# Keeping a twelfth chunk of each row in SBUF between the two layers of a decode attention kernel

## The chip, the core and the metric

The kernel runs on one core of one Trainium2 chip, in one launch. The metric is the device time of that core in microseconds (us), the median of several executions. Less is better.

## What is computed

Two rounds of the same two layers, A then B, on eight rows (a batch of 8, one token each) of 448 numbers. Both rounds of A use the same weights and the same caches.

```python
def _A_ref(x, k_cache, v_cache, wq, wo):        # x 8x1x448, caches 8 x 8 x 4096 x 256
    q = (x @ wq).reshape(B, Sq, 16, 256)...      # 16 query heads, 8 cache heads
    scores = einsum("bhqd,bhkd->bhqk", q, k) * 256 ** -0.5
    p = softmax(scores)
    o = einsum("bhqk,bhkd->bhqd", p, v)
    return o... @ wo
x = x + A(layernorm(x)); x = x + B(layernorm(x))   # B: two small matmuls, gelu, an MLP
x = x + A(layernorm(x)); x = x + B(layernorm(x))
```

Everything is bf16. The caches dominate: 32 MiB for the eight heads of one row, K and V together, 256 MiB for all rows, and each of the two rounds needs all of it. The second round of a row can only begin when the first round of that row, A and B, is done; rows do not depend on each other.

## The kernel before

**Chunks.** A row's heads are taken in four pairs (`gp` 0 to 3). A pair's K is cut into four chunks of 1 MiB, and so is its V: 32 chunks to a row and pass, 512 uses of chunks in all. A chunk is [128 partitions x 4096 bf16]. The first round is pass 0 (`ps == 0`), the second pass 1.

**Places.** SBUF has `NC = 15` places of a chunk's size (one tile, `places_t`, line 76). Every chunk lies in one of them from the issue of its load to its last use.

**Kept chunks.** The list `kept` (lines 63 and 64) names the chunks of each row that stay in their place after their use in pass 0 and are used again in pass 1 without a load: all four K chunks of pairs 3 and 2, and V chunks 1, 2 and 3 of pair 3. That is eleven. Two more are kept outside the places: V chunk 1 of pair 2 (`inner`, line 65) is moved to PSUM by transposes (`away`, line 745) and brought back in pass 1 (`back`, line 752), and a quarter of V chunk 0 of pair 3 (`part`, line 66) lies in PSUM too, so that this load is 768 KB in pass 1.

**Order of the work.** `tasks` (lines 528 to 544) lists pass, row and pair by hand. Row by row it goes: the pairs 3 and 2 of pass 1, in which the kept chunks are used up; then work on other pairs mixed with pairs 2 and 3 of the next row's pass 0, whose chunks now take the places that came free; then the remaining pairs of pass 1 and pairs 0 and 1 of pass 0 of the row after that. `items` (lines 555 to 564) makes one item of each chunk's use: the K chunks of a task alternate with the V chunks of the task before it. `flushed` puts the last four V chunks together before the next row's pass 1 begins.

**Work on a chunk.** For K (lines 876 to 924): DVE transposes it in place in three instructions (`transpose_k`, line 708), and PE computes the scores (`scores`, line 715), 32 matmuls with 128 columns. If both chunks of a couple lie in places next to each other and neither has to be waited for, one set of 32 matmuls with 256 columns does both (`paired`, line 588). ACT takes the exponential (line 737). For V (lines 925 to 960): 16 matmuls into the output bank (`pv`, line 776). Between the items, `step` (line 838) does a piece of the small work of finished rows: softmax sums, output projection, MLP, the next query.

**Loads.** `loads` (line 578) holds the items that need a load, in the order of use: all but the kept and inner ones of pass 1. After each item, the place of its chunk is given back (`places.append`, line 975), unless the chunk stays, and `emit_loads` (line 660) issues as many of the next loads as there are free places, from SP's queue. `place_for` and `both_for` choose the place: for K chunks of a couple they look for two places side by side and may hold one of them back; couples that land in one are loaded by one DMA of 2 MiB (line 675), all others by one of 1 MiB (line 700). Eight semaphores serve the DMAs in turn, so at most eight are under way.

Of the kernel before, what the change touches and what calls it, by code (L numbers as in the profile page):

```python
# [17 lines left out]
def kernel(  # L18
# [37 lines left out]
    GP = G // 2  # L56
# [4 lines left out]
    NC = 15  # L61

    kept = [(gp, 0, n) for gp in (GP - 1, GP - 2) for n in range(4)]
    kept += [(GP - 1, 1, n) for n in range(1, 4)]
    inner = (GP - 2, 1, 1)
    part = (GP - 1, 1, 0)
    Q4 = 4 * Dh
# [791 lines left out]
    for idx, it in enumerate(items):  # L859
# [7 lines left out]
        n, kv, c = it  # L867
# [181 lines left out]
```

## Time and profile before

| | |
|---|---|
| runs | 1097.26, 1099.54, 1105.74 us; median 1099.54 |
| profiled execution | span 1093.6 us from the first to the last instruction; the page gives no other time for it |
| busy, share of the span | PE 62%, weight loads 41%, DVE 55%, ACT 12%, POOL 1% |
| granted TensorE clock | 0.593 of full speed on average |
| moved by DMA | 446.80 MB, 444.32 of it on SP's queue, 1.93 MB in 118 packets of instructions |
| loads of V chunks | 215 of 1024 KB, 8 of 768 KB, 2 of 512 KB |
| loads of K chunks | 146 of 1024 KB, 23 of 2048 KB |
| SP waits before V and K loads for | DVE transposes 203.7 us, PE's V matmuls 180.0 us, PE's score matmuls 102.3 us, landings of V 110.1 us and of K 87.0 us |

A profile here is one execution as the hardware's profiler recorded it. Its page gives the busy time of each engine, and, in 40 equal slices, the busy share of each engine in tenths and what the DMA engines moved. The trace behind it can be asked for any stretch of time, for each issue of a DMA and its landing, and for what ended each wait. PE is TensorE (PEld its weight loads), DVE is VectorE, ACT ScalarE, SP the engine whose queue issues the loads. A line number such as L713 is one of the kernel. When SP waits before a load, the name behind it is the work that had to end first: the last reader of the chunk that was in the place, or the landing of an earlier DMA of the same semaphore.

In the last 30 us of the span the loads have ended; the last chunk lands at 1080.7 us, and the rest is the end of the last row and the output.

### The profile page before, as it was taken

Reading aid. Unit: us, or ns where it says so; the run is one execution under the profiler, and the core shown is the slowest. Engines: PE = TensorE matmul, PEld = TensorE weight load, DVE = VectorE, ACT = ScalarE, POOL = GpSimd, SP = SyncE. Lnnn points to the kernel's source line nnn. Section 1 sums busy time; section 2 is a strip of 40 time slices with the busy share of each in tenths; the row PEclk is TensorE's granted clock in tenths of the full one; section 3 lists DMA queues with packets and bytes.
Section 4 is the critical chain, followed back from the end, with each engine's and each line's share of the span. In section 5 each row is a group of like instructions: output and inputs, shape, how many; then the busy total and the mean of one; then the engine's idle time right before and its main releaser. Section 6 shows DMA issues by size and latency. Waiting matters only on the chain. (4 is left out here: it accounts for less than half of the span.)

```text
span 1093.6 us, 32866 instructions
## 1 busy us (share of the span) xinstructions
PE 674.9 (62%) x15063; PEld 451.8 (41%) x15063; DVE 599.1 (55%) x1215; ACT 125.9 (12%) x362; POOL 16.3 (1%) x27
## 2 busy tenths in 40 slices
PE   3234568456864677446774467834776477767775
PEld 2123345334642355324552245522454244545554
DVE  4256564656366555555465564665637553585462
ACT  0001101110110111101021001201111101111110
POOL 0000000000000000000000000000000000000000
PEclk9986556655575556555566555665556555665565
DMA  9999999999999999999999999999999999999994
GB/s 356 394 427 419 416 403 420 420 416 407 418 423 419 406 417 422 423 419 402 419 422 423 420 401 418 423 421 417 411 416 421 420 398 419 421 411 409 421 417 188
DMA packets 62010, 446.80 MB, mean 409 GB/s; under 512 B 6568, under 2 KB 10544, under 8 KB 12336
## 3 DMA queue, kind: packets, MB, share of 16 engines
q1 hardware_dynamic: 61680, 444.32, 98.6%
q8 instruction: 118, 1.93, 0.7%
q10 hardware_dynamic: 192, 0.38, 0.2%
q14 instruction: 20, 0.16, 0.0%
HBM read 444.67 MB, written 0.01 MB: 407 GB/s over the span
## 5 line engine op out<-in xcount | busy, mean ns | idle before, releaser
L713 DVE STREAM_TRANSPOSE places<-places 128x512 uint32<-128x512 uint32 (+1 forms) x576 | 462.0, 858 | 263.1 <-DMA places<-in_A_k_cache_dram 262.7
L728 PE MATMUL sc<-places,qbd 128*8 128x128 bf16 (+1 forms) x6720 | 281.9, 309 | 217.8 <-DVE places L713 179.7
L783 PE MATMUL o<-places,ptw 128*8 128x256 bf16 x3968 | 241.9, 387 | 144.6 <-DMA places<-in_A_v_cache_dram 122.1
L728 PEld LDWEIGHTS <-qbd 128*8 128x8 bf16 x6720 | 161.2, 101 | 312.8 <-issue 136.8
L783 PEld LDWEIGHTS <-ptw 128*8 128x8 bf16 x3968 | 114.1, 109 | 192.2 <-issue 151.0
L737 ACT ACTIVATE p_n<-sc 128x256 bf16<-128x256 f32 x128 | 95.6, 747 | 763.1 <-PE sc L728 763.1
L309 PEld LDWEIGHTS <-wq_sb 128*128 128x128 bf16 x1152 | 36.0, 104 | 28.3 <-issue 18.4
L358 PEld LDWEIGHTS <-wo_sb 128*128 128x128 bf16 x1280 | 38.4, 102 | 19.8 <-issue 19.8
L332 DVE CAST qbd<-misc 32x64 bf16<-32x64 f32 x64 | 13.8, 216 | 55.6 <-PE misc L328 55.0
L309 PE MATMUL misc<-xb,wq_sb 128*128 128x1 bf16 x1024 | 34.5, 166 | 6.2 <-ACT ptw L771 3.2
L358 PE MATMUL misc<-OT,wo_sb 128*128 128x1 bf16 x1024 | 34.5, 165 | 1.2 <-issue 1.2
L737 ACT ACTIVATION_READ_ACCUMULATOR p_n<-sc 128x1 f32 x128 | 33.9, 265 | 0.0
L771 ACT CAST ptw<-misc 128x128 bf16<-128x128 f32 x64 | 17.4, 273 | 139.1 <-PE misc L764 79.1
L463 PEld LDWEIGHTS misc<-R,o_sb 128*128 128x128 f32 x124 | 26.1, 292 | 9.4 <-issue 8.6
L247 POOL TENSOR_TENSOR t<-t,nhalf 128x2 f32<-128x2 f32 (+2 forms) x20 | 14.0, 703 | 1064.9 <-DVE t L268 1064.9
L463 PE MATMUL misc<-R,o_sb 128*128 128x8 f32 x124 | 28.8, 342 | 0.1
L431 PE MATMUL misc<-zm,one 128*128 128x8 f32 (+1 forms) x66 | 18.5, 354 | 15.0 <-DVE zm L423 14.2
L755 DVE STREAM_TRANSPOSE places<-store 128x512 uint32<-128x512 uint32 x32 | 20.1, 684 | 10.7 <-PE sc L728 10.6
L431 PEld LDWEIGHTS misc<-zm,one 128*128 128x128 f32 x66 | 16.0, 300 | 21.5 <-issue 15.8
L376 PEld LDWEIGHTS <-w_sb 128*128 128x128 bf16 x560 | 17.2, 105 | 9.4 <-issue 9.2
L376 PE MATMUL misc<-xb,w_sb 128*128 128x1 bf16 (+1 forms) x560 | 18.5, 166 | 3.6 <-DVE xb L286 2.2
L748 DVE STREAM_TRANSPOSE store<-places 128x512 uint32<-128x512 uint32 x32 | 19.9, 690 | 0.9 <-DMA places<-in_A_v_cache_dram 0.8
(103 smaller groups left out, 241.9 us busy)
## 6 DMA issues: line engine op xcount, KB each, us to landing
places<-in_A_v_cache_dram SPq DMA_DIRECT2D x215, 1024.0 KB, 9.5
places<-in_A_k_cache_dram SPq DMA_DIRECT2D x146, 1024.0 KB, 9.9
places<-in_A_k_cache_dram SPq DMA_DIRECT2D x23, 2048.0 KB, 18.7
places<-in_A_v_cache_dram SPq DMA_DIRECT2D x8, 768.0 KB, 7.2
wo_sb<-in_A_wo_dram SPq DMA_DIRECT2D x1, 3584.0 KB, 27.5
wq_sb<-in_A_wq_dram SPq DMA_DIRECT2D x3, 1024.0 KB, 8.0
w_sb<-in_B_w_dram SPq DMA_DIRECT2D x1, 1568.0 KB
w_sb<-in_B_w_dram SPq DMA_DIRECT2D x3, 448.0 KB, 26.2
```

The source lines that it names most:

```text
L309: nc.tensor.matmul(q_ps[:, j * Hq + h, :], w, xbs(nb)[:, xi, :], start=(fc == 0), stop=(fc == 3),)
L358: nc.tensor.matmul(y_ps[:, fc, :], w[:, i, at : at + 128], rhs(i), start=start, stop=stop, skip_group_check=open is not None,)
L376: nc.tensor.matmul(h_ps[:, c * nb : c * nb + nb], w, xbs(nb)[:, xi, :], start=(fc == 0), stop=(fc == 3),)
L431: nc.tensor.matmul(z_ps, ones, zm[:], start=True, stop=True)
L463: nc.tensor.matmul(ot_ps[:, j], o_sb[:].rearrange("p (i j) -> p j i", j=2)[:, j], R[:], start=True, stop=True)
L713: nc.vector.transpose(w, w)
L728: nc.tensor.matmul(sc[32 * k : 32 * k + 8, 128 * x : 128 * (x + nx)], qbd[:, ep, gp].rearrange("p a h -> p (a h)"), v, start=(n == 0), sto ...
L737: nc.scalar.activation(p_sb[:, :, :, 2 * u : 2 * u + 2].rearrange("p t i x -> p x t i"), sc[:, 256 * u : 256 * u + 256].rearrange("p (x t ...
L748: nc.vector.transpose(store[n][:].bitcast(U32), slot[:].bitcast(U32)[:, 512 * n : 512 * n + 512])
L755: nc.vector.transpose(slot[:].bitcast(U32)[:, 512 * n : 512 * n + 512], store[n][:].bitcast(U32))
L771: nc.scalar.copy(ptw[:, :, :, 6:8], pt_ps.rearrange("p t k (a h) -> p a (t k) h", a=4),)
L783: nc.tensor.matmul(o_ps[32 * q : 32 * q + 8, :], ptz[:, at : at + 8], v[:, y * Dh : (y + 1) * Dh], start=False, stop=(y >= 12), skip_group ...
```

## The change

V chunk 2 of pair 2 joins the list of kept chunks. For each row it stays in its place from its use in pass 0 to its use in pass 1, and its load in pass 1 is left out. While a row's kept chunks are all there, three of the fifteen places are left for all other chunks instead of four. The lists of tasks and items are the same; the planner assigns places by the same rules to one load fewer for each row.

```diff
     kept = [(gp, 0, n) for gp in (GP - 1, GP - 2) for n in range(4)]
-    kept += [(GP - 1, 1, n) for n in range(1, 4)]
+    kept += [(GP - 1, 1, n) for n in range(1, 4)] + [(GP - 2, 1, 2)]
     inner = (GP - 2, 1, 1)
     part = (GP - 1, 1, 0)
```

## The prediction

> **What bounds the kernel now.** I read three views in this order: the page's slices of time, busy time by stretches, and the DMA issues with their time to landing. The slices first:
>
> ```profile
> DMA  9999999999999999999999999999999999999994
> GB/s 356 394 427 419 416 403 420 420 416 407 418 423 419 406 417 422 423 419 402 419 422 423 420 401 418 423 421 417 411 416 421 420 398 419 421 411 409 421 417 188
> DMA packets 62010, 446.80 MB, mean 409 GB/s; under 512 B 6568, under 2 KB 10544, under 8 KB 12336
> ```
>
> The DMA engines are busy from the first slice to the last but one. No engine of the core is (PE 62%, DVE 55%). So the time is bytes over rate, plus a head and a tail, and a byte not loaded is worth its full transfer. The stretches show where this holds only just:
>
> ```profile
> 300.00:368.00 68.00, 36.08 (x802) 23.25 (x790) 41.14 (x63) 8.31 (x23) 0.00 (x0) 0.63 1.01 421
> 368.00:428.00 60.00, 44.73 (x994) 30.73 (x998) 31.54 (x79) 7.36 (x22) 1.25 (x2) 0.53 1.01 412
> 428.00:500.00 72.00, 35.64 (x766) 22.00 (x755) 43.10 (x65) 8.22 (x23) 0.00 (x0) 0.57 1.01 421
> 500.00:560.00 60.00, 46.15 (x970) 30.78 (x971) 30.65 (x78) 7.65 (x23) 1.26 (x2) 0.52 1.01 411
> ```
>
> The last figure is GB/s, the one before it the DMA share. Each row of the batch has a loose stretch (421) and a tight one (411 to 412). In the tight one all eleven kept chunks are resident and the stream turns in four places. The issues of the same two kinds, from issue to landing, first 375 to 406 us (tight), then 443 to 475 us (loose):
>
> ```profile
> places<-in_A_v_cache_dram SPq DMA_DIRECT2D x7, 1024.0 KB, 8.1
> places<-in_A_k_cache_dram SPq DMA_DIRECT2D x5, 1024.0 KB, 7.3
> ...
> places<-in_A_v_cache_dram SPq DMA_DIRECT2D x5, 1024.0 KB, 23.2
> places<-in_A_k_cache_dram SPq DMA_DIRECT2D x3, 1024.0 KB, 21.2
> ```
>
> Chunks land 2.49 us apart (1 MiB at 421 GB/s), so 21 to 23 us is a queue of eight, and 7.3 is one of three: the fourth place holds the chunk being worked on. How long it is held, for a K chunk that landed at 393.13:
>
> ```profile
> 393.15 2.43 DVE L713 STREAM_TRANSPOSE places<-places 128x1024 uint32<-128x1024 uint32 x3 [1.53 <-DMA places<-in_A_k_cache_dram]
> 395.64 0.39 PE L728 MATMUL sc<-places,qbd 128*8 128x128 bf16 x8 [0.21 <-DVE places L713]
> 396.06 0.33 SPq L700 DMA_DIRECT2D places<-in_A_k_cache_dram  x1
> ```
>
> Three transposes, the last eight score matmuls, and at 396.06 SP issues the next load into the place: 2.93 us after landing. The tight stretches' K chunks give 2.93 to 3.03 nearly always; V chunks 1.1 to 2.9, mostly 2.0 to 2.4.
>
> **The change, removed work.** The chunk (pair 2, V, 2) of each row is no longer loaded in the second pass: 8 loads of 1 MiB, 8.39 MB. The fifteen stretches into which I cut 125 to 1012 us move 408 to 422 GB/s; at 416 that is 20.2 us. The eight SP issues of 0.33 us lie beside transfers and are worth nothing. The 16 matmuls that read the chunk stay. If the gain were all, the time would be 1099.5 - 20.2 = 1079.3.
>
> **The change, one place less.** From the chunk's first use to its second the stream turns in three places instead of four. With four, a load issued at release has until 9.96 us after the old chunk's landing (4 x 2.49); with three, until 7.47. For a place that held K, 7.47 - 2.94 = 4.53 us remain. How long does a 1 MiB load take with nothing ahead of it? The best row is the load issued at 150.19, late because the K chunk before it was held 4.55 us. In the trace its semaphore counts once for each of the 16 DMA engines: twelve had run dry and report 4.37 to 4.83 us after the issue, the other four, still busy, 5.33 to 6.27. A chunk is there when the last of 16 is, so I take 4.85, a little over the last dry one; the low bound is 4.45, near the first of them. Then a K place is late by 2.94 + 4.85 - 7.47 = 0.32 us. A V place held 2.3 us is not late (7.15).
>
> Being late by 0.32 shifts all that follows, and this gives the next K place its time back: with loads counted in order, the one three after a K chunk pays, the one two later just makes it, the next pays again. So I charge every second K. Going through the 16 alternating chunks of the stretch from 368 us with their own hold times, I get 0.39 + 3 x 0.31 = 1.3 us. There are eight such stretches: 10.7 us. The K chunk held 4.55 us in row 0 costs another 1.6 once. Sum 12.3. With 4.45 in place of 4.85 it is about 2 (1.5 once, and little else); if every K pays, 8 x 8 x 0.32 + 1.6 = 22.
>
> The Trainium skill ("DMA: Bandwidth & Descriptors", section "Anatomy of one DMA") puts a DMA at about 2.0 us plus bytes over 436 GB/s, fitted on another issue path; for 1 MiB I estimate 4.4 us from it. That is the first dry engine's row, not the last's: by the rule the K place would be in time and the total would be near 1081, by the row it is late.
>
> **The change, less room for uneven engines.** The page counts 118 instruction packets of 16 KB. Such a packet goes to one of the 16 DMA engines and costs it about two data packets, 2 x 0.311 = 0.62 us. Landings after one come 2.67 to 2.88 us apart instead of 2.49. With four places the engines may drift apart by 9.96 - 2.94 - 4.45 = 2.6 us before those in front run dry, so most of this is absorbed: in the tight stretches landings average 2.52. With three places they are held together within 0.1 us, and a late engine delays all. About five packets fall on the alternating part of each stretch; I take 0.35 each (the landing steps of 0.2 to 0.4), 1.75, less 0.5 paid already (16 x 0.03): 1.25, times eight is 10 us. Bounds: nothing, and the full 0.62 on each, 8 x 3.1 - 4 = 21. The sign cannot turn: less slack makes no transfer earlier.
>
> **The change, the rest.** Nothing is moved in PE's, DVE's or ACT's order, and no queue gets an instruction more. After the stretch, four V chunks in a row are held 1.1 to 2.1 us and are in time with three places; then second-pass chunks free places without loads. The planner will place chunks differently, and a K pair that is no longer adjacent takes 64 narrow score matmuls for 32 wide ones. That happens in loose stretches, where PE is busy 36 of 68 us: nothing. Without that cover it would be 2 x 1.07 - 1.88 = 0.26 us per pair.
>
> **Sum.** The profiled execution's span is 1093.6 us; the page gives no other time for it, and the runs shown (1097.26 to 1105.74) are 3.7 to 12.1 longer, the median 5.9. The terms change the span: 1093.6 - 20.2 + 12.3 + 10 = 1095.7; plus 5.9 is 1101.6, which I round to 1102.
>
> **Rivals.**
> *The gain comes through.* Three places are enough: the load takes 4.45, uneven engines are caught up in the idle moments of late loads. For it: the V places have 0.3 us or more to spare, the tight stretches today lose nothing in landings (2.52 against 2.51 in the loose ones). Against it: the twelve dry engines. 1099.5 - 20.2 + 2 = 1081, or 1085 with a third of the unevenness. Chance 0.19.
> *Slower: the engines in lockstep.* With no slack, each instruction packet on any engine holds up all 16 by its full 0.62, and the shift no longer falls on the places that had time to spare, so every K pays. For it: eight K chunks at the limit per stretch. Against it: late loads leave idle time in which a late engine catches up. 1099.5 - 20.2 + 22 + 21 = 1122. It decides once a stretch loses over 20.2 / 8 = 2.5 us, one transfer; over 1% slower from 3.9 us. Chance 0.24.
> *The engines become the bound.* In the tight stretch PE is busy 45 and DVE 32 of 60 us; there is room. It would show as longer holds, and give 1102 and more. Chance 0.03, on the slow side.
> *It doesn't do what it says.* The load list leaves out second-pass items of kept chunks, so eight loads go. If not, 1122. Chance under 0.01.
>
> **How the numbers follow.** My forecast has the remaining 0.54. A measurement of this kernel can tell about 1% from no change: 1088.5 and 1110.5. Of the first rival nearly all lies below 1088.5, 0.17. Of the second and third rival most lies above 1110.5; with the forecast's upper tail (full cost of one of the two terms, 1112) this is 0.27. The rest, 0.56, is within 1%. For eight in ten I cut about a tenth at each end: 1085 to 1118. The forecast's own range is 1092 to 1111.
>
> **What would show it.** Bytes: the main queue at 435.9 MB instead of 444.3, V loads of 1024 KB down from 215 to 207. Tight stretches: time to landing after a K place 4.5 to 5.5 us instead of 7.3, median of V below 6; GB/s there under 405, the DMA share below 1.00, packets missing every fourth chunk. Loose stretches unchanged at 421. Wrong would be: tight stretches still at 411 (first rival), below 390 (second), holds of K over 3.2 us (third), or a loss in the loose stretches, for which I have no term.

## The result, and the profile after

The changed kernel takes 1161.59 us (median of 4 runs, 1156.79 to 1171.84), against 1098.40 for the kernel before beside it: a ratio of 1.057, 95% interval 1.050 to 1.063. The forecast was 1102, with a range to 1118. The profiled execution has a span of 1157.8 us, and the page of the kernel after says of its DMA:

```profile
DMA  9999999999999999999999999999999999999994
GB/s 355 397 426 420 368 330 394 423 371 348 366 423 421 373 357 399 423 420 356 361 418 421 396 349 328 422 421 386 359 342 421 397 335 340 421 363 346 337 415 197
DMA packets 61431, 438.36 MB, mean 379 GB/s; under 512 B 6504, under 2 KB 10480, under 8 KB 12272
...
q1 hardware_dynamic: 61104, 435.93, 95.4%
```

The bytes are those announced: the main queue moved 435.93 MB instead of 444.32. The DMA line still shows nines, so it hides the loss; the GB/s line shows it. Fourteen slices stand at 415 to 426 as before; between them lie groups, one for each row, that have fallen from 400 to 420 to as little as 328. Busy time by stretches, loose and tight in turn, with the DMA share and GB/s last:

```profile
306.00:380.00 74.00, 44.08 (x900) 28.07 (x896) 45.16 (x69) 10.24 (x29) 0.00 (x0) 0.55 1.01 416
380.00:452.00 72.00, 49.41 (x1010) 32.66 (x1006) 34.51 (x86) 8.11 (x24) 1.25 (x2) 0.50 0.96 367
452.00:520.00 68.00, 33.31 (x766) 21.07 (x758) 41.78 (x63) 8.30 (x23) 0.00 (x0) 0.65 1.01 422
520.00:585.00 65.00, 43.63 (x903) 28.44 (x903) 29.25 (x76) 7.32 (x22) 1.25 (x2) 0.50 0.95 363
```

The loose stretches move 416 to 422 GB/s as before. The tight ones moved 411 to 412 and now move 363 to 367. Against the bound on record (under 390 speaks for the second rival) that is far below. PE and DVE have no more to do there than before (49.41 and 34.51 of 72 us), so no engine of the core has become the bound.

The issues of the tight stretch from 386 to 446 us, to landing:

```profile
places<-in_A_v_cache_dram SPq DMA_DIRECT2D x12, 1024.0 KB, 6.4
places<-in_A_k_cache_dram SPq DMA_DIRECT2D x10, 1024.0 KB, 7.4
```

I expected 4.5 to 5.5 us after a K place, as an empty queue gives, and a median under 6 for V. They take 6.4 and 7.4 (8.1 and 7.3 before), although a whole chunk less lies ahead of them. And the hold of a K chunk (from its landing to the issue of the next load into its place) is what it was, here for one that landed at 547.27 us:

```profile
547.29 2.43 DVE L713 STREAM_TRANSPOSE places<-places 128x1024 uint32<-128x1024 uint32 x3 [1.96 <-DMA places<-in_A_k_cache_dram]
...
549.78 0.39 PE L728 MATMUL sc<-places,qbd 128*8 128x128 bf16 x8 [0.21 <-DVE places L713]
...
550.21 0.33 SPq L700 DMA_DIRECT2D places<-in_A_v_cache_dram  x1
```

The next load into its place is issued 2.94 us after the landing, as before (2.93). So the work on a chunk has not become slower; the loads have.

**Where the time went.** I followed every single load of 1 MiB in the eight tight stretches. A chunk should land 2.49 us after the one before it, or 4.72 us after its own issue (an empty DMA queue, measured below), whichever is later. Issues that came too late for the first explain 5.4 us in all. Landings later than both make 87.9 us, against 6.4 in the kernel before, so 81.5 more. So: 1093.6 - 20.2 + 5.4 + 81.5 = 1160, against a span of 1157.8. The question is what the 81.5 us are.

The 16 reports of the DMA engines (the counts of the load's semaphore, us after its issue) show who is late. Three loads of the kernel after:

```
issue 544.62 (V)   4.30 4.31 4.34 4.34 4.36 4.38 4.43 4.46 4.49 4.51 4.52 4.72 4.80  5.76 5.77 6.19
issue 550.21 (V)   4.61 4.68 4.72 4.77 4.79 4.83 4.84 4.86 4.88 4.96 5.08 5.17 5.25  5.75 6.15 7.08
issue 692.76       12 between 4.50 and 4.72                                          5.73 5.76 7.66 9.25
```

Most engines report as early as from an empty queue, and three or four come 1 to 4.5 us later. A chunk is there only when the last has reported. Part of this delay is plain: those engines were still at work on the load before, which landed 2.65, 3.08 and 5.30 us after these issues. Beyond the plain step the three chunks are late by 1.06, 1.51 and 1.47 us.

### The profile page after: what moved, and what is told of

It is laid out like the page before. It is cut to its first block, busy times and chain, and to the rows that moved or that the text cites. A ratio compares the mean times of both kernels' runs of the same rounds, so it can differ in the third digit from the quotient of the medians.

```text
span 1157.8 us, 32144 instructions
## 1 busy us (share of the span) xinstructions
PE 673.1 (58%) x14679; PEld 444.0 (38%) x14679; DVE 599.3 (52%) x1215; ACT 126.0 (11%) x362; POOL 16.3 (1%) x27
## 3 DMA queue, kind: packets, MB, share of 16 engines
q1 hardware_dynamic: 61104, 435.93, 95.4%
## 5 line engine op out<-in xcount | busy, mean ns | idle before, releaser
L783 PE MATMUL o<-places,ptw 128*8 128x256 bf16 x3968 | 238.6, 385 | 181.6 <-DMA places<-in_A_v_cache_dram 164.6
L728 PEld LDWEIGHTS <-qbd 128*8 128x8 bf16 x6336 | 153.5, 101 | 348.4 <-issue 140.0
L748 DVE STREAM_TRANSPOSE store<-places 128x512 uint32<-128x512 uint32 x32 | 19.9, 690 | 1.0 <-DMA places<-in_A_v_cache_dram 0.9
```

The lines of the kernel that those rows point to most:

```text
L728: nc.tensor.matmul(sc[32 * k : 32 * k + 8, 128 * x : 128 * (x + nx)], qbd[:, ep, gp].rearrange("p a h -> p (a h)"), v, start=(n == 0), sto ...
L748: nc.vector.transpose(store[n][:].bitcast(U32), slot[:].bitcast(U32)[:, 512 * n : 512 * n + 512])
L783: nc.tensor.matmul(o_ps[32 * q : 32 * q + 8, :], ptz[:, at : at + 8], v[:, y * Dh : (y + 1) * Dh], start=False, stop=(y >= 12), skip_group ...
```

## The experiments

The theory on record when they began: the number of places alone costs it, and the loss grows with the hold, since three places leave no slack and the last engine of a load reports only some 6 us after the issue. From the loads alone on it is split in two (A: as in the forecast, by instruction packets that delay single engines; B: by engines restarting unevenly after their queue ran empty, without any such packet). Rival: the longer residence changes the planner's placing, and so PE's work. Later the runs led to D and E, told below. In the tables "step" is the mean time between landings.

**Is it the number of places?** The kernel before, with one place less and nothing else kept:

```diff
-    NC = 15
+    NC = 14
```

> The kernel before with 14 places instead of 15: eleven kept chunks, so three places for the stream as in the changed kernel, but all loads of the kernel before. Theory (three places do not cover a K chunk's 2.94 us of work plus a load whose last DMA engine reports some 6 us after the issue): the changed kernel's loss without its saving, 1161.6 + 20.2 = 1182 us, within 15; loads 2.8 us apart in the tight stretches. Rival (the twelfth kept chunk itself, its place and the couples that the planner forms around it, cost the time): near 1098, at most 1110.

1182.99 us, ratio 1.076 (1.073 to 1.079): 83.1 us for the place alone, as the theory had it; the rival, which gave at most 1110, is out. With the 20.2 saved that makes +62.9, and the change made +63.2. Its page shows the same groups of slow slices:

```profile
GB/s 355 398 425 421 374 325 381 421 379 330 343 423 421 366 330 389 424 419 354 341 386 423 418 358 361 422 422 402 343 346 423 387 359 349 422 396 347 346 413 204
```

**Does the saving come out if the place is given back?** The kernel after with 16 places, so that four remain for the stream. Memory for it comes from a weight that is not loaded (`w4`, 1.6 MB; `w3` is read in its stead), so this is no version to use:

```diff
-    NC = 15
+    NC = 16
...
-    w4_sb = consts.tile([128, HC, D], BF16, name="w4_sb")
+    w4_sb = w3_sb[:].rearrange("p (c d) -> p c d", d=D)
...
-    nc.sync.dma_start(w4_sb[:], B_w4.rearrange("(c p) d -> p c d", p=128))
```

> The changed kernel with a sixteenth place, so twelve kept chunks and four places for the stream. To find room, the weights w4 are not loaded and w3 is used where they stood (1.6 MB less, 3.8 us). Theory: the saving comes out and nothing else, 1098.4 - 20.2 - 3.8 = 1074 us, within 5; landings 2.52 us apart. Rival (the kept chunk or the planner's couples): the loss stays, about 1155.

1079.46 us, ratio 0.980 (0.977 to 0.983), 20.5 us below the kernel before. On record were 24.0 (20.2 for the eight loads, 3.8 for `w4`), so the eight loads gave 16.7 us if `w4` is counted in full, and 20.5 if not at all. The slices are fast again:

```profile
GB/s 353 406 426 420 411 393 416 421 413 401 415 422 421 405 406 423 423 420 406 390 422 422 421 393 403 419 423 412 407 414 421 416 404 407 420 388 411 406 420 176
```

The two terms are now separate: a saving of 17 to 20 us and a price of 83 for the fourth place. With three places the saving shows without `w4`: the kernel with 14 places lies 83.1 us above the kernel before and the changed one 63.2, so the same eight loads are worth 19.9. In the other direction, a fifth place (ten kept chunks, eight loads more):

```diff
-    kept += [(GP - 1, 1, n) for n in range(1, 4)]
+    kept += [(GP - 1, 1, n) for n in range(1, 3)]
```

> The kernel before with ten kept chunks (V chunk 3 of pair 3 is loaded again), so five places for the stream. Both theories (a stream that is short of places; single DMA engines that fall behind): eight transfers more and nothing gained, 1099 + 20 = 1119 us, within 5, since the tight stretches with four places land 2.52 us apart against 2.51 in the loose ones. If four places already cost something, less: 1105 to 1115.

1115.57 us, ratio 1.013 (1.011 to 1.015). The eight loads should cost 20.2, so the fifth place gives back about 5: four places are nearly free of the loss, three are deep in it.

**Is it the hold of K?** The kernel after with the first of the three transposes only (the scores are then of partly untransposed K):

```diff
-        for e0, e1 in ((0, 2), (2, 3), (3, 4)):
+        for e0, e1 in ((0, 2),):
```

> The changed kernel, but K chunks get one transpose (half the chunk) instead of three, so that the scores are computed from a half transposed K. A K place is then held about 2.94 - 1.22 = 1.7 us. Theory: 1.7 + 5.9 - 7.47 is 0.1 us late at a K place instead of 1.4, so most of the loss goes: 1078 to 1100 us. Rival (kept chunk or couples): at least 1150. If a V place with its 2 us is as late as a K place, something between, about 1125.

1156.77 us, ratio 1.053 (1.049 to 1.056): nothing gained. The hold fell less than meant, to 2.4 to 2.8 us, since the scores now run after the transpose. But half a microsecond less on every K chunk should have freed what theory A and the forecast charge for lateness. A miss for both. The time is what the rival (the planner's placing) gave, at least 1150, but the run with 14 places had ruled that rival out.

Also K chunks loaded as two DMAs of 512 KB, each half transposed as it comes, on the kernel after and, as a control, on the kernel before:

```diff
-            if loads:
+            if loads and not kv:
+                for y in range(2):
+                    nc.sync.dma_start(
+                        dst[:, 8 * Dh * y : 8 * Dh * (y + 1)], src[:, 8 * Dh * y : 8 * Dh * (y + 1)]
+                    )
+            elif loads:
...
```

> The changed kernel, but each K chunk loaded alone comes by two DMAs of 512 KB (its two halves of 8 rows of 512 B a partition), and is transposed in six instructions, the first three as soon as the first half is there. The hold after the last landing falls from 2.94 to about 1.7 us. If the hold decides: 1080 to 1100 us. If it does not (the run with one transpose left the time at 1157): 1140 to 1165.

> The same two edits on the kernel before, with four places: the control for the halves. No change, 1095 to 1104 us, if transfers of 512 KB run at the same rate; 1110 or more if eight DMAs under way are then too few for the loose stretches.

1157.78 us, ratio 1.051 (1.048 to 1.054), and 1105.33, ratio 1.004 (1.002 to 1.005). No help with three places, although two K places near 400 us were held only 1.86 and 2.25 us after the last landing; a small cost with four.

**The loads by themselves.** A kernel that does nothing but load chunks into four to one places and read them, first with the transposes and matmuls, then with a tiny copy only:

> No attention at all: only 1 MiB loads of K and V in turn, into 4, 3 and 2 places with three transposes and 5 matmuls on a K chunk and 16 matmuls on a V chunk before its place is loaded again (48, 48, 32 chunks), then into 3, 2 and 1 places with only a tiny read in between (32, 32, 24 chunks). Hardly any instructions are fetched. Theory (the last of 16 engines is late of itself): one place 5.5 to 6 us from issue to landing; 4 places 2.5 us a chunk, 3 places 2.75 to 2.9, 2 places 4 or more. Rival (packets of instructions make single engines late): one place 4.5 to 5.0 us, 3 places 2.50 to 2.60.

| places, work | hold, us | step, us | issue to landing, us |
|---|---|---|---|
| 4, transposes and matmuls | 2.0 to 4.9 | 2.81 | |
| 3, the same | | 3.08 | |
| 2, the same | | 4.30 | 4.61 to 4.90 |
| 3, tiny copy | 0.29 | 2.49 | |
| 2, tiny copy | 0.29 | 2.58 | 4.82 |
| 1, tiny copy | 0.29 | 5.04 | 4.59 to 5.02, median 4.72 |

The lowest row is the clean measurement of a load with all 16 engines idle: the last reports at 4.72 and never after 5.02. My 4.85 was right, and the 5.5 to 6 us that the theory on record had for this row are out. PE was slower there than in the kernel, so the sections with work had other holds (K 3.2 to 3.9 us) and say little. The next run sets the holds by instructions on memory of their own, and adds suspects one by one:

> Loads alone again, K and V in turn, with holds that touch the places as little as possible: for K about 2.9 us on ScalarE on other memory, for V about 1 to 2 us on GpSimd on other memory. Stretches of 40 chunks: 4 places; 3 places; 3 places with 32 tiny matmuls a chunk beside it (instructions are fetched as in the attention kernel); 3 places with the real transposes of K in the hold; 4 places with the tiny matmuls. Theory A (packets of instructions make single engines late, and with three places every engine waits for them): 2.50 to 2.60, 2.52 to 2.65, 2.8 to 2.9, 2.55 to 2.65, 2.52 us a chunk. Theory B (hold and restart after an empty ring are enough): 2.50, 2.8 to 2.9, 2.8 to 2.9, 2.8 to 2.9, 2.50. Theory C (the transposes disturb the transfers): only the stretch with real transposes is at 2.8 to 2.9.

| places; K held 3.04 us, V 1.34 | step, us | instruction packets |
|---|---|---|
| 4 | 2.51 | |
| 3 | 3.09 | 0 |
| 3, with 32 tiny matmuls a chunk | 2.94 | 10 |
| 3, with the real transposes | 3.16 | |
| 4, with the tiny matmuls | 2.55 | 10 |

So the loss is there without any instruction packet, without matmuls and without transposes: 0.60 us on every chunk. Theory A, which was my second rival's mechanism, is out as the cause. B stands, though it had 2.8 to 2.9 where 3.09 was measured.

**When does an engine fall behind?** All holds equal, from short to long:

> Loads alone, every chunk held alike, the hold made by ScalarE and VectorE in turn on other memory. Two places with holds of 0.3, 0.8, 1.2, 1.6, 2.0, 2.4, 2.8, 3.4, 4.2 us, then three places with 0.3, 1.0, 1.7, 2.4, 3.0 us; 24 chunks each. Theory D (a DMA engine whose ring was empty for a short time starts its next packets late, up to 3 us, and one such engine holds up the chunk): two places give 2.5 to 2.6 us a chunk at 0.3, then more than (hold + 4.72) / 2 by 0.4 to 1 us in the middle of the row, 1.6 to 2.8, and the plain (hold + 4.72) / 2 again at 3.4 and 4.2 (4.06, 4.46), where the rings are long empty; three places 2.49 up to 1.7, 2.8 or more at 2.4 and 3.0. Theory E (hold and a load of 4.72 us add up, no engine restarts late): the larger of 2.49 and (hold + 4.72) / 2 everywhere with two places (2.51, 2.76, 2.96, 3.16, 3.36, 3.56, 3.76, 4.06, 4.46), and 2.49, 2.49, 2.49, 2.49, 2.57 with three.

| places | hold, us: step, us |
|---|---|
| 2 | 0.3: 2.58, 0.8: 2.88, 1.2: 3.07, 1.6: 3.26, 2.0: 3.49, 2.4: 3.63, 2.8: 3.90, 3.4: 4.18, 4.2: 4.66 |
| 3 | 0.3: 2.49, 1.0: 2.56, 1.7: 2.81, 2.4: 3.24, 3.0: 2.78 |

With two places the steps are the plain (hold + load) / 2 all along: (2.55 + 4.8) / 2 = 3.67 at 2.4, 3.63 measured. Engines that ran empty long ago restart in time. So both theories on record for this run missed: D expected 0.4 to 1 us beyond the plain step in the middle of the row with two places, E at most 2.57 with three. With three, 2.4 us is *worse* than 3.0. What answers to this is not the hold but how much of the earlier work was left when the next load was issued. With three places, 2 x 2.49 - 2.4 = 2.6 us are left at a hold of 2.4, and 1.6 to 2.0 at the longer ones (3.0 to 3.4 as measured). In the section with 2.4 the reports are (us after issue):

```
issue 1001.80   4.39 4.40 4.49 4.50 4.53 4.54 4.54 4.55 4.58 4.58 4.66 4.67 4.67 4.72 4.73  7.68
issue 1004.02   4.80 4.81 4.81 4.82 4.85 4.88 4.89 5.01 5.04 5.15 5.43 5.46 5.48 5.74 5.79  8.14
issue 1006.70   4.57 4.61 4.62 4.63 4.65 4.75 4.75 4.76 4.81 5.18 5.28 5.50 5.56 6.74 6.97  7.99
issue 1011.92   4.26 4.29 4.32 4.35 4.37 4.41 4.42 4.50 4.53 4.54 4.55 4.67 4.69 4.70 4.73  7.71
```

At 1011.92 fifteen engines had run empty and report in 4.26 to 4.73. The last one was busy until 1014.69 with the load before; it should have gone on and reported 2.49 later, at 1017.18. It reports at 1019.63, another 2.45 us later. And since its report is the landing that sets the next issues, it finds itself in the same position again. (The reports do not name their engine; that it is the same one is inferred from the steps.)

The trace's packet records show what the late engine does. An engine's share of a load is eight packets of 8 KB, 0.309 us each as a rule. The last engine ends its share of the load before at 1014.40 (its report follows at 1014.69). From about 1014.5 to 1015.8 only 15 engines (14 for a moment) have a packet under way, while the other 15 are at their shares of the load issued at 1011.92 and the last one's share of it is still to come. So it stands still for over 1 us with work queued, and that share is the one reported at 1019.63.

Theory D from here on: a load issued when some 2 to 3.4 us of work are left catches some engines at a bad moment and costs up to a full transfer more; issued earlier or later it does not. Its rival E: three places are too few, and a longer hold is always worse. Two predictions of D are odd enough to test: a longer hold makes the kernel faster, and four places go bad when a hold brings them to the same moment.

In the kernel after, GpSimd reads each V chunk too, around a power on scratch data, so that its place is held 2.95 us (3.0 in the trace); then V to 3.3 and K, which was meant to be held 3.3 too but measured 3.05; and the same on the kernel before:

```diff
+    def hold_on(slot, n):
+        two = hs[:, 16:17].bitcast(BF16)
+        nc.gpsimd.tensor_copy(two, slot[:, 0:2])
+        nc.gpsimd.tensor_tensor(hs[:, 0:n], hs[:, 0:n], hs[:, 0:n], ALU.pow)
+        nc.gpsimd.tensor_copy(two, slot[:, 2:4])
...
+                if not stays(it) and items[idx - 1][1] == 0:
+                    hold_on(slot, 14)
                 pv(st["o", g8], slot, c, gp)
```

> Changed against the kernel after: each V chunk of the stream that follows a K chunk is also read by GpSimd, before and after a power of 14 elements in a scratch tile of its own, so that its place is given back about 2.95 us after landing instead of 1.1 to 2.2; nothing else is changed and all is computed. Two theories, after the sweep of holds, in which three places cost 3.24 us a chunk at a hold of 2.4 and only 2.78 at a longer one of 3.0. D (an unlucky moment): what counts is how much of the work issued earlier is still under way when a load is issued. In the traces so far the landing step has its plain length (2.49, or the issue plus 4.72) where under 1.8 us or over 4.2 us are left, and is up to 1.5 us longer on average in between; a V place given back after 1.3 us leaves 3.6, one given back after 2.95 leaves 2.0, at the edge. So a longer hold makes the kernel faster: 1105 to 1145, and below 1150 in any case, against 1161.6. E (the gap): each time the engines run empty some restart late, and a longer hold makes more such times: 1165 to 1185.

> As e10_v_held, with a power of 16 elements for V (hold about 3.3 us) and a power of one element for K after its transposes (hold about 3.3 instead of 2.94); all is computed. Then under 1.8 us of work are left at each issue. By the plain arithmetic of hold plus 4.72 three places now lose 5.1 us a stretch, against 1.5 at the usual holds. D: that loss and nearly nothing more: 1079.5 + 4 + 8 x 5.1 = 1124, with 0.06 us a chunk left over 1136; 1115 to 1145, faster than the kernel after although each place is held longer. E: what the kernel after has, and 8 x 3.7 = 30 us more: about 1190.

> The same two additions on the kernel before, with its four places; all is computed. Control for what GpSimd's instructions cost by themselves. At each issue 7.47 - 3.3 = 4.2 us are left, at the far edge of the bad zone. D: 1100 to 1115. E: 1099 to 1103, since no engine runs empty. Over 1120 would say that the additions themselves cost time and the two runs before say less.

With V held: 1147.53 us, ratio 1.042 (1.037 to 1.047), so 14 us faster than the kernel after although every V place that follows a K chunk is held longer; E had expected slower. The intervals of the two ratios do not overlap. The time is below D's bound of 1150 and 2.5 us above D's range. With K held too: 1160.20, ratio 1.053 (1.047 to 1.058). This is a miss for D (1115 to 1145) and for E (about 1190). The reason shows in the trace: a landing that is late once shifts the distances, so that the issues of that run have between 1.0 and 5.4 us left and not the 1.7 I had counted on; 111 of its 205 single loads lie between 2.2 and 4.2. The control with four places: 1116.35, ratio 1.012 (1.008 to 1.016), a little over D's 1115 and above E's 1103. There the V holds of 3.3 leave about 4.2, and the K holds of 3.05 about 4.4. How much of the 13.5 us is the price of the added instructions is not separated.

The last run brings four places to the moment by longer holds, and tries two queues in the sections at the end:

> Loads alone, 28 of 1 MiB in each of 14 sections; the output is not computed. Each place is held for one set time, by a copy and a memset or copy of other memory, on VectorE, ScalarE and GpSimd in turn. Four places with holds of 2.4, 3.0, 3.6, 4.2, 4.8, 5.4, 6.0; three with 1.3, 2.1, 2.7, 3.3; three with the V loads issued from ScalarE's queue and the K loads from SyncE's, 1.3, 2.1, 2.7. With the work left at an issue as the plain landing steps give it (2.49 times the places less one, less the hold): four places 5.1, 4.5, 3.9, 3.3, 2.7, 2.1, 1.5 us; three places 3.7, 2.9, 2.3, 1.7. D (an unlucky moment): it is the work left, not the number of places: four places show 2.5 up to a hold of 3.0, then longer steps, at most 2.8 to 3.3 at holds of 4.2 to 4.8, and at 6.0 about the plain (6.0 + 4.72) / 4 = 2.68, so less than the worst; three places 2.8 to 3.2 at 2.1 and 2.7, and 2.7 at 3.3. E (three places are too few, or a longer hold is always worse): four places stay at 2.5 to 4.8 and then rise steadily to 2.68. Two queues: if the late restart belongs to one queue's list on an engine, the steps are 2.5 to 2.55 there; if to the engine itself, 2.8 to 3.2 as with one queue.

| places | hold, us (left, us): step, us |
|---|---|
| 4 | 2.4 (5.1): 2.49, 3.0 (4.5): 2.51, 3.6 (3.9): 2.50, 4.2 (3.3): 2.89 |
| 3 | 1.3 (3.7): 2.56, 2.1 (2.9): 2.87, 2.7 (2.3): 3.38, 3.3 (1.7): 2.70 |
| 3, two queues | 1.3: 2.71, 2.1: 3.09, 2.7: 3.44 |

The busy time of the stretches of four of these sections, with GB/s last (four places at 3.6 and 4.2, three at 2.7 and 3.3):

```profile
139.00:210.00 71.00, 32.88 (x30) 31.59 (x28) 29.64 (x27) 1.00 1.01 419
212.00:290.00 78.00, 38.12 (x30) 33.98 (x26) 33.72 (x26) 1.00 0.98 370
...
721.00:812.00 91.00, 19.51 (x27) 23.56 (x27) 22.15 (x26) 1.00 0.86 322
818.00:892.00 74.00, 24.46 (x27) 28.14 (x26) 24.56 (x24) 1.00 0.98 387
```

Four places lose 50 GB/s between a hold of 3.6 and one of 4.2, where (4.13 + 4.72) / 4 = 2.21 would still leave 2.49 a step: the number of places is not the cause. Three places win 65 from 2.7 to 3.3. (In the four-place sections of 4.8, 5.4 and 6.0 some places were held up to 10.9 us, where VectorE fell behind: one of its tiny copies took 4.11 us. So their steps of 2.88, 3.09 and 3.31 are not those of the set holds, and D's 2.68 at 6.0 is untested.)

Two queues do not help, and they do not in the kernel. V loads from ScalarE's queue, from GpSimd's, and from ScalarE's in the kernel before:

```diff
-                nc.sync.dma_start(dst[:, z0:], src[:, z0:])
+                (nc.scalar if kv else nc.sync).dma_start(dst[:, z0:], src[:, z0:])
```

> The kernel after, with the single V loads issued from ScalarE's queue instead of SyncE's; everything is computed. If the late restart belongs to one queue's list: 1080 to 1105. If it belongs to the engine: 1150 to 1170. A cost of its own is possible on top: ScalarE waits for the place before each V load, and the exponentials behind it wait too.

> The same with GpSimd's queue in place of ScalarE's, where little else waits; everything is computed. One queue's list: 1080 to 1110. The engine: 1150 to 1170. Issuing there may take longer, which would show in the time from issue to landing.

> The kernel before, with its four places, and the single V loads issued from ScalarE's queue; everything is computed. Control for what the second queue costs by itself: 1095 to 1105 in either theory if it costs nothing.

1178.67 (ratio 1.071, 1.066 to 1.077), 1196.32 (1.087, 1.082 to 1.092), and 1142.86 for the control (1.038, 1.031 to 1.044). All three miss the ranges on record. A second queue costs 41 us even with four places, where one tight stretch now moves 373 GB/s instead of 412:

```profile
368.00:428.00 60.00, 38.08 (x840) 26.19 (x843) 27.30 (x68) 5.39 (x16) 1.25 (x2) 0.50 0.95 373
```

The Trainium skill ("DMA: Bandwidth & Descriptors", section "Queues, rings and completion order") says that each pair of a queue and a DMA engine is a ring of its own. The idea that the late restart belongs to such a ring found no support in these four results; it is not excluded by them, since the second queue has a price of its own that they do not separate.

**All loads together.** For each single load of 1 MiB (and, in the kernels, the eight of 768 KB): "left" is the landing of the load before it less its own issue; "late" is its step beyond the larger of 2.49 and 4.72 - left. Loads alone are those of one queue in e8 (its first two sections), e9 and e13; of the kernels those between 60 and 1100 us with up to 7 us left; number and mean late in us:

| left, us | loads alone | kernel before | kernel after | after with V held |
|---|---|---|---|---|
| under 1.8 | 122: 0.04 | 0 | 1: 0.97 | 7: 0.73 |
| 1.8 to 2.2 | 70: 0.22 | 0 | 16: 0.77 | 26: 0.35 |
| 2.2 to 2.6 | 84: 0.39 | 0 | 16: 1.26 | 39: 0.63 |
| 2.6 to 3.0 | 48: 1.00 | 1: 0.84 | 14: 1.17 | 9: 0.56 |
| 3.0 to 3.4 | 34: 0.84 | 0 | 13: 1.03 | 32: 0.33 |
| 3.4 to 3.8 | 29: 0.27 | 0 | 19: 0.50 | 24: 0.27 |
| 3.8 to 4.2 | 89: 0.10 | 1: 0.46 | 29: 0.28 | 15: 0.13 |
| over 4.2 | 244: 0.02 | 184: 0.02 | 96: 0.06 | 59: 0.05 |

This is the answer to where the time went. The kernel before issues all but two of these loads with more than 4.2 us left. The kernel after issues 107 with 1.8 to 4.2 left, and these are late by 79.9 us in all, of the 87.9.

The run with V held does not fit so simply. It has 80 loads with 2.2 to 3.4 us left, where the kernel after has 43, but they are late by 0.33 to 0.63 us instead of 1.03 to 1.26. So its gain came, but not in the way D gives, which was fewer loads in the zone; what made them less late is not shown.

The packet records also split the loss. In the tight stretches from 380 to 452 and from 520 to 585 us, 181 and 186 of some 3000 packets of 8 KB took more than 0.45 us, most of them the first of an engine's share; in the kernel before (368 to 428 and 500 to 560) 39 and 31 did. The mean rose from 0.32 to 0.34 us. This makes about half of the 11 to 12% of the rate that were lost. The other half is time in which an engine has no packet at all: the DMA share fell from 1.01 to 0.96 and 0.95.

## Why the prediction was wrong, point by point

- *The removed work, 20.2 us:* right. With three places it is 19.9 us; with four, 16.7 to 20.5.
- *A load on an empty queue, 4.85 us:* right (4.72, at most 5.02), and it decided nothing here. The estimate from the Trainium skill ("DMA: Bandwidth & Descriptors", section "Anatomy of one DMA"), a fit for another issue path, was 4.4 us, 0.3 less.
- *The hold, 2.94 us:* right (2.94), and no engine of the core became slower.
- *Late K places, 12.3 us:* right in kind, too much in size: 5.4 us measured.
- *Less room for uneven engines, 10 us, at most 21:* this is the step that failed. It measured 81.5 us, about 10 in each stretch where I had 1.25. I took the five instruction packets of a stretch as the only thing that sets one engine back, and bounded the term by their 0.62 us each. (That price was too low: the median record of such a packet in the trace before is 1.07 us. With it the bound would have been 39, still under half.) Loads alone lose 0.60 us a chunk without one such packet. Single engines fall behind without it, by 2.45 us in the load shown, when a load is issued with some 2 to 3.4 us of work left. The three-place stream, with holds of 1.1 to 2.9 us, issued 43 of 204 loads with 2.2 to 3.4 us left and 107 with 1.8 to 4.2; the kernel before issued two.
- *The sentence "less slack makes no transfer earlier", with "most of this is absorbed":* right for four places, but I read the calm of the kernel before as a property of the engines. It went with the moment of its issues.
- *The row I had in hand:* the load issued at 150.19, from which I took 4.85. It is the one load of the kernel before with 2.94 us left, and its four other engines reported at 5.33 to 6.27. I wrote that they were "still busy" and left them out, although I wrote beside it that a chunk is there when the last of 16 is. The last was at 6.27: the chunk landed 0.84 us later than the plain step. Charging 0.84 for each of the 107 loads with 1.8 to 4.2 us left gives 90 us. The count is known only now and 0.84 is one load, so that this comes near is partly luck; but the row showed that there was a price, and I used its fast end.
- *Rivals:* the second (slower, "lockstep") had the sign and the place, tight stretches only, but its price was 1122 and its cause, the instruction packets, was not needed. The first and third are refuted by the GB/s and the holds. Loose stretches were unchanged, as expected.

What stays open: why a DMA engine stands still, or takes longer over its first packet, in that moment. Instruction packets, transposes and matmuls are each shown not to be needed, and four places lose too at a hold of 4.2. Whether the queue plays a part is not shown. The amount left is shown to order the lateness, but it is not the whole of it: two places at a hold of 0.3 have 2.2 us left and their steps were only 0.1 over the plain, and with V held the loads between 2.2 and 3.4 were late by half of what they are in the kernel after. No version that computes everything beat the kernel before; e2 beats it by 2% only because it leaves out a weight, and its 16 places do not fit beside that weight.

## What to carry to other kernels

When a stream of large loads gets one buffer less, do not only ask whether a load on an empty queue arrives in time; ask how much work is left in the queue at each issue, and look in the trace of before for loads issued with as much left as the new ones will have. Here over 4.2 us left was safe and 1.8 to 3.4 cost 0.8 to 1.3 us a load, in all four times what the saved bytes were worth. Take the last of the 16 engines' reports as the duration of a load, never the first twelve, and treat the one row in which the queue nearly ran dry as the price and not as an exception.

## What the runs showed of the hardware that was not expected

- A DMA engine that is still at work, with 2 to 3.4 us left when the next load of 1 MiB is issued, can be late with its part, by 2.45 us in the load shown, and stands still for over 1 us of that; engines that are already idle report in 4.3 to 4.8 us.
- So the time is not monotonic in the hold: three places, step 3.38 us at a hold of 2.7 and 2.70 at 3.3; and the kernel after became 1.2% faster when its V places were held longer.
- The DMA busy share shows only about half of this loss: 0.95 to 0.96 in the tight stretches instead of 1.01, and nines in every slice but the last, at 363 to 367 GB/s instead of 411 to 412. A packet that takes 0.6 to 1 us instead of 0.309 counts as busy.
- Issuing the single V loads from a second queue made the kernel before 3.8% slower.
